# Transformer block with its backward pass on one core: order and pacing of the projection work beside the first chunk of attention

## The chip, the core and the metric

The kernel runs on one core of a Trainium2 chip. The core has five engines that each work through their own instruction list in order and wait for one another by semaphores: PE (TensorE, matmuls and transposes; its weight loads are shown as PEld), DVE (VectorE), ACT (ScalarE), POOL (GpSimd) and SP (SyncE, which here only starts transfers). POOL starts transfers too. The metric is device time in microseconds (us), the median of several runs; lower is better.

## The reference

The program computes one block (attention, then an MLP with squared ReLU, both with adaptive layer norm) and the gradients of all its parameters and of its input. What matters here is the attention of the forward pass: 2048 tokens, width 512, 32 heads of width 16.

```python
qkv = (x @ wqkv).reshape(B, S, 3, H, Dh).transpose(2, 0, 3, 1, 4)
q, k, v = (qkv[0], qkv[1], qkv[2])
scores = jnp.einsum('bhqd,bhkd->bhqk', q, k) * scale
p = _softmax(scores, axis=-1)
o = jnp.einsum('bhqk,bhkd->bhqd', p, v)
...
h = _layernorm(x, axis=-1) * (1 + ca) + sa
x = x + ga * _A_ref(h, A_wqkv, A_wo)
```

Its gradient needs Q, K and V again, in two layouts: with the head channels on the partitions ("feature-major", written by the projections) and with the tokens on the partitions ("token-major", or, for V, the reverse turn). So each projected block is also turned by PE transposes and stored in device memory for the backward pass.

## The kernel before

**Steps and units.** The forward attention goes through chunks of 512 queries (`qc`, 4 of them), in each through 8 groups of four heads (`g`), in each through two pairs of heads (`jp`). One (`qc`, `g`, `jp`) is a unit, numbered `n`; the first chunk is units 0 to 15. A unit has 16 steps (`kb`), one for each block of 128 keys. A step is: two score matmuls on PE into a PSUM tile `st` (L388), one exponential of 128x1024 on ACT into `pu` (L391), and eight small matmuls `pv` of an earlier step on PE into `accbank` (L322). `st` has two buffers.

**Background work.** Only units 0 and 1 have their Q and K ready when attention starts. The others are projected during the first chunk by `gen_qkv` (L663), a Python generator that emits a few PE matmuls and yields what they cost. After each step of units 2 to 15 `bg.step(1.2)` (L405) advances it: it adds 1.2 to a credit (at most 2) and runs the generator until the credit is used up. What the generator yields decides the pacing:

- a number is a price, taken off the credit;
- a tuple stops this step's work. `("wait", n)` also sets `hold` to n, and the next n steps then run no background at all and add no credit (L65 to L67);
- a tuple such as `(g, 0)` or `(-g, 0)` is a mark as well.

`bg.until(mark)` (L382, L408) runs the generator until it passes the mark, whatever that costs, between two steps. It is called twice for each group of heads: in the second unit of group g, ahead of step 5, until the first block of Q of group g+1 is projected (mark g+1); and at the end of that unit until all of K of group g+1 is (mark -(g+1)). In this document such a run between two steps is called a burst. `bg.drain()` (L371) at the end of the first chunk runs what is left.

**What the generator does for a group.** Q block 0, four K blocks (into the tile `KTq` that the next group's scores read), then, for some groups, extra work: the turns of a scaled weight `wm_s` (`gen_turn`, groups 4 to 7), or of V (`gen_vt`, groups 3 to 6), or the modulation rows (`gen_mod`, group 2). Then Q blocks 1 to 3 of the group before.

**One block** is `gen_fm` (L623): four matmuls into a PSUM tile `pps` (L630, a yield of 1 after each of the first three), the evacuation by DVE (L637, "CAST", into `ev_fm` or `KTq`), a store on SP's queue (L641), and then `token_major` (L643): four transposes of that same block into another `pps` tile (L717), its copy by DVE into `ev_tm` (L720), and a store on POOL's queue (L647 for K; L650 and L652 for Q). Between the evacuation and the turn stands `yield ("wait", 1)` (L659). `pps` has two buffers (`self.mps`). For the blocks projected during units 0 and 1 the turns are put in a list, `late`, and done one per step at the start of unit 2.

**V** (`gen_vt`, L694): four token blocks, each padded into a tile `vpad` (a DVE memset of a column of ones, L703, then two POOL `tensor_scalar`, L704 and L705), then `("wait", 3)` (L706), then eight transposes, a copy into `vT`, and after the fourth a store (L708). The column `one` has two buffers.

**Queues.** The orders of PE, ACT, DVE and SP are as the Python code emits them; POOL's order in this stretch is set by a scheduler. `load_q` (L299) loads the next unit's queries on POOL's queue (L302); it comes right after the burst ahead of step 5.

Of the kernel before, what the change touches and what calls it, by code (L numbers as in the profile page):

```python
# [10 lines left out]
F32 = mybir.dt.float32  # L11
ACT = mybir.ActivationFunctionType
ALU = mybir.AluOpType
# [6 lines left out]
P = 128  # L20
DH = 16
# [14 lines left out]
class Background:  # L36
# [13 lines left out]
    def next(self):  # L50
        while self.gens:
            r = next(self.gens[0], None)
            if r is not None:
                if isinstance(r, tuple):
                    self.mark = r[0]
                    self.seen.add(r[0])
                return r
            self.gens.pop(0)
        return None
# [46 lines left out]
class K:  # L106
# [160 lines left out]
    def phase_fwd(self):  # L267
# [66 lines left out]

        KT = kp.tile([P, S], BF16, name="KTq")
        self.late = []
# [3 lines left out]
        QTo = []  # L340
        first = self.gen_open(Vaug, KT, QTm, QTo, stp, bg)
        next(first)
# [5 lines left out]
        for i, (n, kb) in enumerate(units):  # L348
# [4 lines left out]
            for a in range(2):  # L353
                nc.tensor.matmul(stt[:, a, :], lhsT=KT[:, kb * P:(kb + 1) * P], rhs=(QTm[2 + a] if n else QTo[a])[:],
                                 start=True, stop=True)
# [11 lines left out]
        bg.until(-1)  # L367
        KT = self.KT_next
        for n, (qc, g, jp) in list(enumerate(order))[2:]:
# [9 lines left out]
            for kb in range(ST):  # L379
# [7 lines left out]
                for a in range(2):  # L387
                    nc.tensor.matmul(stt[:, a, :], lhsT=KT[:, kb * P:(kb + 1) * P], rhs=QTm[2 * jp + a][:],  # L388
                                     start=True, stop=True)
# [16 lines left out]
            if jp == 1 and n + 1 < len(order):  # L406
                if n < 2 * NQ - 1:
                    bg.until(-(g + 1))  # L408
                KT = KTn
        bg.until(f"fc2_{SC - 2}")  # L410
# [212 lines left out]
    def gen_fm(self, ps, t, g, s0, dst=None, masked=None):  # L623

        nc = self.nc
        DT, NQ = self.DT, self.NQ
        eb = self.qkv_eb
        pt = ps.tile([P, 512], F32, name="pps")
        for kt in range(DT):
            nc.tensor.matmul(pt[:], lhsT=self.wpads[t][:, kt, g, :] if g else self.wpad0[t][:, kt, :], rhs=self.xm1T[:, kt, s0:s0 + 512],  # L630
                             start=(kt == 0), stop=(kt == DT - 1))
            if kt < DT - 1:
                yield 1
        if dst is None:
            ev = eb.tile([P, 512], BF16, name="ev_fm")
            dst = ev[:]
        nc.vector.tensor_copy(dst, pt[:])  # L637
        if masked:
            for j in range(4):
                (nc.scalar.copy if j == 1 else nc.vector.tensor_copy)(masked[j][32 * j:32 * j + 32, :], ev[32 * j:32 * j + 32, :])  # L640
        nc.sync.dma_start((self.QTq_d, self.KTq_d)[t][g, :, s0:s0 + 512], dst)  # L641

        def token_major():  # L643
            tm = eb.tile([P, 4, 4, 32], BF16, name="ev_tm")
            self.turn_now(tm[:].rearrange("p s j e -> p s (j e)"), dst, 4)
            if t:
                nc.gpsimd.dma_start(self.ktm_d[g, :, s0:s0 + 512], tm[:].rearrange("p s j e -> p (s j e)"))  # L647
                return
            tmc = eb.tile([P, 4, 4, DH], BF16, name="ev_tmc")
            nc.gpsimd.tensor_copy(tmc[:], tm[:, :, :, 0:DH])  # L650
            w = 4 * DH
            nc.gpsimd.dma_start(self.qtm_d[g, :, s0 // P * w:(s0 // P + 4) * w],  # L652
                                tmc[:].rearrange("p s j d -> p (s j d)"))

        if self.late is not None:
            self.late.append(token_major)
            yield 1
            return
        yield ("wait", 1)  # L659
        token_major()  # L660
        yield 1.5

    def gen_qkv(self, kp):  # L663

        nc = self.nc
        S, NQ, ST = self.S, self.NQ, self.ST
        for g in range(1, NQ):
            while self.cur_g < g - 1:
                yield ("wait", 0)
            KT = self.KT_next = kp.tile([P, S], BF16, name="KTq")  # L670
            yield from self.gen_fm(self.mps, 0, g, 0)
            yield (g, 0)
            for s0 in range(0, S, 512):
                yield from self.gen_fm(self.mps, 1, g, s0, dst=KT[:, s0:s0 + 512])
            yield (-g, 0)
            if 3 < g <= 3 + self.DT:
                wt = self.qkv_eb.tile([P, 3 * self.DT, P], BF16, name="wm_t", bufs=1)
                yield from self.gen_turn(wt[:], w[:], 3 * self.DT)
                nc.gpsimd.dma_start(self.WmT_d[g - 4], wt[:].rearrange("p n k -> p (n k)"))
            if 2 < g < 3 + self.DT:  # L680
                w = self.qkv_eb.tile([P, 3 * self.D], BF16, name="wm_s", bufs=2)
                sc = self.qkv_eb.tile([P, 1], F32, name="wm_c", bufs=2)
                nc.vector.tensor_copy(sc[:], self.opcaT[:, g - 3:g - 2])
                nc.gpsimd.tensor_scalar(w[:], self.wq[:, g - 3, :], sc[:], 1.0, ALU.mult, ALU.mult)
            if g == 2:
                yield from self.gen_mod()
            elif 3 <= g < 3 + self.SC:
                yield from self.gen_vt(4 * (g - 3))
            for s0 in range(512, S, 512):
                yield from self.gen_fm(self.mps, 0, g - 1, s0)  # L690
        for s0 in range(512, S, 512):
            yield from self.gen_fm(self.mps, 0, NQ - 1, s0)

    def gen_vt(self, s0):  # L694

        nc = self.nc
        NQ = self.NQ
        vT = self.qkv_eb.tile([P, NQ, 4 * P], BF16, name="vT", bufs=1)
        for k in range(4):
            vp = self.vpads[k]  # L700
            v = self.Vaug[:, s0 + k, :, 0:DH].rearrange("p (g j) d -> p g j d", j=4)
            one = self.qkv_eb.tile([P, 1], F32, name="one", bufs=2)
            nc.vector.memset(one[:], 1.0)  # L703
            nc.gpsimd.tensor_scalar(vp[:, :, 0:2, 0:DH], v[:, :, 2:4, :], one[:], 1.0, ALU.mult, ALU.mult)  # L704
            nc.gpsimd.tensor_scalar(vp[:, :, 2:4, 0:DH], v[:, :, 0:2, :], one[:], 1.0, ALU.mult, ALU.mult)  # L705
            yield ("wait", 3)  # L706
            yield from self.gen_turn(vT[:, :, k * P:(k + 1) * P], vp[:].rearrange("p g j e -> p (g j e)"), NQ)
        nc.gpsimd.dma_start(self.VTq_d.rearrange("g p s -> p g s")[:, :, s0 * P:(s0 + 4) * P], vT[:])  # L708

    def gen_turn(self, dst, src, n, pool=None, name="pps", copies=None):  # L710
# [1291 lines left out]
```

## Time and profile before

| | us |
|---|---|
| median of 3 runs (3242.07 to 3249.86) | 3242.19 |
| the profiled execution: its own time | 3241.86 |
| its span, first to last instruction | 3240.1 |
| PE busy | 3034.6 (94%) |
| ACT busy | 2818.9 (87%) |
| DVE busy | 2140.4 (66%) |
| POOL busy | 753.1 (23%) |
| ACT exponentials of L391, 992 of them | 912.8 |
| idle time of ACT just ahead of them | 69.0 |

The profile is of one execution; its own time is 0.33 us below the median. A busy PE is not PE at its peak, since matmuls overlap and their ends are modelled. The change touches only the stretch from the start of unit 2 (the first exponential of L391 starts at 64.21 us) to the end of unit 15 (the next unit's first one starts at 341.10 us); shares over the whole span say little about it.

### The profile page before, as it was taken

The page shows a single profiled execution, that of the slowest core. Times are in us where ns is not written, and L with a number is a line of the kernel's source. Part 1 is how long each engine was busy: PE and PEld are TensorE (multiplying, and loading weights), DVE is VectorE, ACT ScalarE, POOL GpSimd, SP SyncE. Part 2 cuts the span into 40 slices and gives each one's busy share as a digit, 9 for nine tenths or more (in the row PEclk, how much of TensorE's full clock was granted, in tenths as well). Part 3 has the DMA queues.
Part 4 walks back from the last instruction along what each step waited for, and adds up shares of the span by engine and source line. Part 5 has one row for each costly group of instructions (what it writes and reads, how often), then busy time and mean ns, then how long its engine had stood idle before and what let it go on. Part 6 is the DMA issues. An engine that isn't in the chain of part 4 may idle for free.

```text
span 3240.1 us, 86820 instructions
## 1 busy us (share of the span) xinstructions
PE 3034.6 (94%) x35635; PEld 1580.3 (49%) x35879; DVE 2140.4 (66%) x4195; ACT 2818.9 (87%) x4259; POOL 753.1 (23%) x1337
## 2 busy tenths in 40 slices
PE   8888999999999699999999999999999999999998
PEld 4544555555555248444444444444444444444443
DVE  6333223312332657588888888888888888888867
ACT  7876999999999045499999999999999999999965
POOL 3233511211121213421221122122212221221122
PEclk9999999999999899999999999999999999999999
DMA  4122401311221334400000000000000000000033
GB/s 150 60 70 96 134 19 61 99 47 32 101 69 36 99 100 148 142 22 11 12 13 12 13 13 12 13 13 13 13 12 13 13 12 13 13 11 14 20 99 116
DMA packets 76933, 158.53 MB, mean 49 GB/s; under 512 B 15140, under 2 KB 41126, under 8 KB 76534
## 3 DMA queue, kind: packets, MB, share of 16 engines
q0 software_dynamic: 38720, 104.04, 10.3%
q1 hardware_dynamic: 35734, 47.88, 4.5%
q8 instruction: 280, 4.59, 0.6%
q10 hardware_dynamic: 2080, 1.05, 0.1%
q14 instruction: 119, 0.97, 0.1%
HBM read 88.41 MB, written 64.49 MB: 47 GB/s over the span
## 4 chain that ended last, share of the span: by engine, by line
PE 32%; issue 30%; ACT 24%; POOL 8%; DVE 5%; DMA 0%; POOLq 0%; DVEq 0%; ACTq 0%; SPq 0%
ACT pu L391 21%; PE st L1642 5%; POOL ds L1577 4%; PE dp L717 3%; DVE ds L1562 3%; PE st L388 3%; PE st L717 2%; PE acckv L1495 2%; PE dps L1024 1%; PE accbank L322 1%; PE dps L1080 1%; PE accq L1520 1%; PE pps L630 1%; PE dp L1695 1%; PE st L1790 1%
## 5 line engine op out<-in xcount | busy, mean ns | idle before, releaser
L1562 DVE TENSOR_TENSOR ds<-dp,pu 128x512 bf16<-128x512 f32 x1888 | 1226.0, 685 | 137.4 <-PE dp L1558 98.7
L1645 ACT ACTIVATE pu<-st 128x512 bf16<-128x512 f32 x2048 | 1116.5, 611 | 43.9 <-PE dp L1558 15.7
L391 ACT ACTIVATE pu<-st 128x1024 bf16<-128x1024 f32 x992 | 912.8, 1081 | 69.0 <-PE st L388 67.5
L717 PEld LDWEIGHTS <-ds 128*128 128x128 bf16 x8192 | 461.0, 98 | 334.4 <-issue 282.0
L388 PE MATMUL st<-QTm,KTq 128*128 128x512 bf16 x1823 | 552.7, 377 | 37.3 <-ACT pu L391 3.9
L322 PEld LDWEIGHTS <-pu 128*128 128x128 bf16 x8192 | 342.8, 96 | 225.5 <-issue 2.3
L720 ACT COPY dsT<-st 128x1024 bf16<-128x1024 bf16 x416 | 427.2, 1027 | 18.4 <-PE st L717 12.1
L717 PE MATMUL dp<-ident,ds 128*128 128x128 bf16 x4096 | 340.6, 221 | 29.7 <-POOL ds L1577 29.0
L322 PE MATMUL accbank<-Vaug,pu 128*128 128x17 bf16 x8192 | 357.6, 171 | 9.8 <-ACT Vaug L521 1.1
L1577 POOL TENSOR_TENSOR ds<-csq,pu 128x512 bf16<-128x512 f32 x128 | 147.6, 1153 | 939.1 <-ACT csq L1576 939.1
L1642 PE MATMUL st<-kvm,QTg 64*128 64x512 bf16 x1024 | 333.2, 382 | 12.2 <-ACT dsT L720 6.9
L1642 PE MATMUL st<-kvm,q 64*128 64x512 bf16 x1024 | 332.7, 383 | 9.8 <-ACT dsT L720 5.6
L1558 PE MATMUL dp<-kvm,q 64*128 64x512 bf16 x1024 | 337.6, 383 | 1.0 <-PE st L1642 0.7
L1558 PE MATMUL dp<-kvm,dOTg 64*128 64x512 bf16 x1024 | 337.5, 382 | 0.0
L720 DVE COPY dsT<-dp 128x1024 bf16<-128x1024 bf16 x416 | 286.5, 689 | 60.1 <-PE dp L717 49.7
L717 PE MATMUL st<-ident,ds 128*128 128x128 bf16 x4096 | 318.1, 221 | 0.1
L388 PEld LDWEIGHTS <-KTq 128*128 128x128 bf16 x1984 | 186.8, 96 | 157.4 <-issue 122.4
L1495 PE MATMUL acckv<-ds,Qg 128*16 128x512 bf16 x1024 | 175.8, 382 | 0.0
L1495 PE MATMUL acckv<-pu,q 128*16 128x512 bf16 x1024 | 175.8, 382 | 0.0
L1495 PE MATMUL acckv<-ds,q 128*16 128x512 bf16 x1024 | 175.8, 382 | 0.0
L1495 PE MATMUL acckv<-pu,dOg 128*16 128x512 bf16 x1024 | 175.8, 382 | 0.0
L302 POOL DMA_DIRECT2D QTm<-QTq_d x124 | 63.1, 510 | 369.2 <-PE st L388 351.3
(442 smaller groups left out, 3797.2 us busy)
## 6 DMA issues: line engine op xcount, KB each, us to landing
KTq<-KTq_d POOLq DMA_DIRECT2D x24, 512.0 KB, 3.8
duT_d<-auT POOLq DMA_DIRECT2D x3, 1792.0 KB, 7.3
aT_d<-rT POOLq DMA_DIRECT2D x3, 1792.0 KB, 12.2
tm_st<-duT_d SPq DMA_DIRECT2D x14, 384.0 KB, 3.5
tm_st<-aT_d SPq DMA_DIRECT2D x14, 384.0 KB, 3.3
KTq_d<-KTq SPq DMA_DIRECT2D x32, 128.0 KB, 1.8
QTq_d<-ev_fm SPq DMA_DIRECT2D x32, 128.0 KB, 1.9
ktm_d<-ev_tm POOLq DMA_DIRECT2D x32, 128.0 KB, 2.1
```

The source lines that it names most:

```text
L302: nc.gpsimd.dma_start(QTm[j][32 * j:32 * j + 32, :], self.QTq_d[g, 32 * j:32 * j + 32, 512 * qc:512 * (qc + 1)])
L322: nc.tensor.matmul(acc[:, a, sub, :], lhsT=pu[:, a, sub * P:(sub + 1) * P], rhs=Vaug[:, kb, h, :], start=(kb == 0 and a == 0 and sub == 0) ...
L388: nc.tensor.matmul(stt[:, a, :], lhsT=KT[:, kb * P:(kb + 1) * P], rhs=QTm[2 * jp + a][:], start=True, stop=True)
L391: nc.scalar.activation(pu[:], stt[:], ACT.Exp, scale=self.scale)
L717: nc.tensor.transpose(pt[:, i, :], src[:, (b0 + i) * P:(b0 + i + 1) * P], self.ident[:])
L720: (copies or [nc.vector.tensor_copy])[b0 // 8 % len(copies or [0])](dst[:, b0:b0 + m, :], pt[:, :m, :])
L1495: nc.tensor.matmul(acckv[r:r + DH, :], lhsT=T[n][:, ib, col:col + DH], rhs=src[:, a, :], start=(ib == 0), stop=(ib == ST - 1))
L1558: nc.tensor.matmul(dp[:], lhsT=T["dOT"][rd, ib * P:(ib + 1) * P], rhs=masked["VT"][a][rd, 512 * c:512 * (c + 1)], start=True, stop=True)
L1562: nc.vector.tensor_tensor(dsg[:, i, a], dp[:], pu[:, a, :], ALU.mult)
L1577: nc.gpsimd.tensor_tensor(dsg[:, i, 1], f[:], pu[:, 1, :], ALU.mult)
L1642: nc.tensor.matmul(stt[:], lhsT=T["QT"][rs, q], rhs=masked["KT"][a][rs, c0:c0 + 512], start=True, stop=True)
L1645: nc.scalar.activation(pu[:, a, :], stt[:], ACT.Exp, scale=self.scale)
```

## The change

- In `gen_fm` the `("wait", 1)` is gone. Instead there is a `yield 1`, and then the turn of the block *before* this one is emitted (`turn_before`, which keeps one open turn in `tm_open`); this block's own turn follows after the next block's projection.
- The last open turn is emitted at the end of `gen_qkv`.
- The padding of V moves out of `gen_vt` into `pad_v`, which pads all four blocks at once and is called for groups 3 to 6 at the start of the group's work, ahead of the projection of Q block 0. The four `("wait", 3)` are gone.

```diff
@@ -656,18 +656,27 @@
             self.late.append(token_major)
             yield 1
             return
-        yield ("wait", 1)
-        token_major()
-        yield 1.5
+        yield 1
+        yield from self.turn_before(token_major)
+
+    def turn_before(self, nxt):
+
+        for f in self.tm_open:
+            f()
+            yield 1.5
+        self.tm_open = [nxt] if nxt else []
 
     def gen_qkv(self, kp):
 
         nc = self.nc
         S, NQ, ST = self.S, self.NQ, self.ST
+        self.tm_open = []
         for g in range(1, NQ):
             while self.cur_g < g - 1:
                 yield ("wait", 0)
             KT = self.KT_next = kp.tile([P, S], BF16, name="KTq")
+            if 3 <= g < 3 + self.SC:
+                self.pad_v(4 * (g - 3))
             yield from self.gen_fm(self.mps, 0, g, 0)
             yield (g, 0)
             for s0 in range(0, S, 512):
@@ -690,12 +699,11 @@
                 yield from self.gen_fm(self.mps, 0, g - 1, s0)
         for s0 in range(512, S, 512):
             yield from self.gen_fm(self.mps, 0, NQ - 1, s0)
-
-    def gen_vt(self, s0):
+        yield from self.turn_before(None)
+
+    def pad_v(self, s0):
 
         nc = self.nc
-        NQ = self.NQ
-        vT = self.qkv_eb.tile([P, NQ, 4 * P], BF16, name="vT", bufs=1)
         for k in range(4):
             vp = self.vpads[k]
             v = self.Vaug[:, s0 + k, :, 0:DH].rearrange("p (g j) d -> p g j d", j=4)
@@ -703,8 +711,14 @@
             nc.vector.memset(one[:], 1.0)
             nc.gpsimd.tensor_scalar(vp[:, :, 0:2, 0:DH], v[:, :, 2:4, :], one[:], 1.0, ALU.mult, ALU.mult)
             nc.gpsimd.tensor_scalar(vp[:, :, 2:4, 0:DH], v[:, :, 0:2, :], one[:], 1.0, ALU.mult, ALU.mult)
-            yield ("wait", 3)
-            yield from self.gen_turn(vT[:, :, k * P:(k + 1) * P], vp[:].rearrange("p g j e -> p (g j e)"), NQ)
+
+    def gen_vt(self, s0):
+
+        nc = self.nc
+        NQ = self.NQ
+        vT = self.qkv_eb.tile([P, NQ, 4 * P], BF16, name="vT", bufs=1)
+        for k in range(4):
+            yield from self.gen_turn(vT[:, :, k * P:(k + 1) * P], self.vpads[k][:].rearrange("p g j e -> p (g j e)"), NQ)
         nc.gpsimd.dma_start(self.VTq_d.rearrange("g p s -> p g s")[:, :, s0 * P:(s0 + 4) * P], vT[:])
 
     def gen_turn(self, dst, src, n, pool=None, name="pps", copies=None):
```

## The prediction

> **What bounds the kernel now.** First the page's costliest groups. The exponential of the forward attention is one of them, and it is the only large group that stands idle for PE's score matmuls rather than the other way round:
>
> ```profile
> L391 ACT ACTIVATE pu<-st 128x1024 bf16<-128x1024 f32 x992 | 912.8, 1081 | 69.0 <-PE st L388 67.5
> ```
>
> So ACT sets the pace of the forward attention, and 69.0 us of it is lost waiting for scores. Second, the timeline of ACT alone, which tells where (start, duration of the run of exponentials, and in brackets the idle time ahead of it):
>
> ```profile
> 136.96 19.36 ACT L391 ACTIVATE pu<-st 128x1024 bf16<-128x1024 f32 x21 [3.44 <-PE st L388]
> 164.31 10.19 ACT L391 ACTIVATE pu<-st 128x1024 bf16<-128x1024 f32 x11 [8.00 <-PE st L388]
> 177.95 19.36 ACT L391 ACTIVATE pu<-st 128x1024 bf16<-128x1024 f32 x21 [3.44 <-PE st L388]
> 207.84 10.19 ACT L391 ACTIVATE pu<-st 128x1024 bf16<-128x1024 f32 x11 [10.53 <-PE st L388]
> 221.70 19.36 ACT L391 ACTIVATE pu<-st 128x1024 bf16<-128x1024 f32 x21 [3.68 <-PE st L388]
> 252.85 10.19 ACT L391 ACTIVATE pu<-st 128x1024 bf16<-128x1024 f32 x11 [11.79 <-PE st L388]
> 266.72 19.36 ACT L391 ACTIVATE pu<-st 128x1024 bf16<-128x1024 f32 x21 [3.68 <-PE st L388]
> 296.61 10.19 ACT L391 ACTIVATE pu<-st 128x1024 bf16<-128x1024 f32 x11 [10.53 <-PE st L388]
> 310.47 29.44 ACT L391 ACTIVATE pu<-st 128x1024 bf16<-128x1024 f32 x32 [3.68 <-PE st L388]
> 341.10 79.12 ACT L391 ACTIVATE pu<-st 128x1024 bf16<-128x1024 f32 x86 [1.19 <-PE st L388]
> ```
>
> The counts alternate, 21 steps and 11 steps: every gap lies at a burst, at the end of a unit or ahead of step 5, and between bursts ACT runs without a break at 0.92 us a step (19.36 / 21). Two more such gaps lie earlier, 3.23 us ahead of 100.18 us and 3.22 us ahead of 123.29 us. The twelve add up to 66.4 us: all that the change can win. The rest (1.8 us in unit 2, 0.3 us at the modulation columns) is not of bursts. Third, the timeline of all engines inside the burst ahead of 164.31 us:
>
> ```profile
> 157.25 0.40 PE L717 MATMUL pps<-ident,ev_fm 128*128 128x128 bf16 x4 [0.79 <-DVE ev_fm L637]
> ...
> 157.48 1.03 PE L630 MATMUL pps<-xm1T,wpad 128*128 128x512 bf16 x4
> 157.69 0.42 DVE L720 COPY ev_tm<-pps 128x512 bf16<-128x512 bf16 x1 [0.49 <-PE pps L717]
> 158.18 0.40 POOL L650 COPY ev_tmc<-ev_tm 128x256 bf16<-128x256 bf16 x1 [0.59 <-DVE ev_tm L720]
> 158.55 0.69 DVE L637 CAST ev_fm<-pps 128x512 bf16<-128x512 f32 x1 [0.44 <-PE pps L630]
> 158.87 0.57 POOL L652 DMA_DIRECT2D qtm_d<-ev_tmc  x1 [0.29 <-POOL ev_tmc L650]
> 159.30 0.40 PE L717 MATMUL pps<-ident,ev_fm 128*128 128x128 bf16 x4 [0.79 <-DVE ev_fm L637]
> ...
> 159.53 1.03 PE L630 MATMUL pps<-xm1T,wpad 128*128 128x512 bf16 x4
> ```
>
> A block in a burst is a chain: four matmuls 1.03, then 0.79 in which PE waits for the evacuation, then 0.23 until the next block starts (157.25 to 157.48): 2.05 us, as 157.48 to 159.53 shows.
>
> **Prices.** A 512-column matmul starts 0.217 us after the one before ((1.03 - 0.383 of a single one) / 3); the last one's end lies 0.17 beyond the next start. Eight `pv` less are worth 8 x 0.026 = 0.21 (nine last 0.38, one 0.17). From the build's order of PE instructions I took what each burst holds. The one ahead of 136.96 us holds three matmuls, turn, four matmuls, turn: 0.81 + 0.79 + 0.23 + 1.03 + 0.79 + 0.23 = 3.88, and ACT lost 3.44. So a burst's chain costs ACT itself less 0.44 (what lies ready in `st`); with two matmuls for three (3.67 - 0.44 = 3.23) it gives the 3.22 measured. Where the burst's step has one `pv` and not nine, less 0.65.
>
> **Part 1: no holds.** The holds go (one skipped step per block, three per V block), and each block is charged 1 credit more (5.5 for 4.5). In the built order the bursts shrink: where one held up to four blocks of Q and 16 transposes of V, it now holds two or three blocks. The work that leaves them lies in steps. There it must fit under ACT's 0.92. Summed by the prices above (0.43 for the scores, 0.026 a `pv`, 0.217 a matmul, 0.23 four transposes), the 20 steps ahead of each step-5 burst of groups 3 to 6 come to 16.0 to 16.9 us of PE against 18.4 of ACT, where they were 14.0 to 14.3; the fullest stretch is units 4 and 5 at 18.1. The densest stretch of before, ten steps at 8.80, ran with ACT never idle. I cost the move at 0; without that slack every us moved would come back.
>
> **Part 2: turns one block late.** In a burst the turn of the last block fills PE's wait for this block's evacuation, and the next block's matmuls wait for that evacuation because `pps` has two buffers: 1.03 + 0.79 = 1.82 a block, so 0.23 saved each. Larger is the end: after the last block PE issues its four matmuls (0.87) and an older turn (0.23), waits for nothing, and goes on with the scores. In the built order those scores wait only for their `QTm` loads, as the last K block is read 12 steps later. A burst "three matmuls, turn, four, turn" now costs 0.81 + 0.79 + 0.87 + 0.23 - 0.44 = 2.26; a third block adds 1.82: 4.08.
>
> The sum over the twelve bursts of the built order: six of two blocks 13.6; three of three blocks (ahead of step 5 in groups 4, 5, 6 of the list) 12.3; one with two matmuls first and one `pv` 1.84; the first, four matmuls and a turn, 0.87 + 0.23 - 0.65 = 0.45; the drain, two turns with nothing to wait for, 0. Together 28.1. Saved 66.4 - 28.1 = 38.3.
>
> **Part 3: padding ahead of Q block 0.** In DVE's built order four memsets now stand between the copy of the last turn and the evacuation of Q block 0, the last in its burst. The column `one` has two buffers, so the fourth memset waits until POOL has padded the second block. POOL, from the end of that copy: 0.07 and L650 0.40; L704 0.48; the transfer L652 0.57, which the scheduler put between; L705 0.48; L704 and L705 again 0.93: about 2.95, and with the memset (0.06 and the signal) 3.1. Counted from when PE has issued the next-to-last block, that copy ends at 1.35 (0.21 + 0.69 + 0.03 + 0.42), so the last evacuation starts at 4.45 where it would have at 2.04 (0.96 + 0.87 + 0.21): 2.4 late. Behind it on DVE waits the copy of the burst's own turn (nobody is near it) and on PE the first K matmul, one step on, which needs that `pps` buffer: PE stands from about 2.7 to 5.2, `st` runs dry, and ACT, due at 3.6, goes on at 6.05. That is 2.45 us in each of four bursts: 9.8. Moved past on POOL: L650, L652 and two L302 of the next queries, and on SP the Q store; chain 3.1 + 0.7 + store 1.9 + issue 1.0 + landing 2.0 = 8.7, while PE needs the queries 11 steps later (10.1) and after two more stalls. Cost 0, until that chain grows by some 5 us. The padding is off V's own turns, which come 12 to 17 steps later, and takes with it the 1.9 us that PE waited for POOL in the last V block of three bursts (counted in the 66.4). Lower end of this term 0 (the evacuation not held); upper end 17.6, if the evacuation waited for all eight pads (four more at 0.48, 4.4 each).
>
> **The clock.** PE has waited for POOL before, three times alike, and once the granted clock fell to half:
>
> ```profile
> PE pps L717 <- POOL vpad L705: 5.8, 3, 1.9
> 242.30:245.00 2.70, 2.70 (x12) 1.24 (x12) 0.69 (x1) 0.00 (x0) 0.68 (x1) 0.50 0.00 0
> ```
>
> That burst cost 11.79 against 10.53 for the same work: 1.26. Four new waits, longer than 1.9, at one in three give 1.7; bounds 0 and 5.0. The Trainium skill ("TensorE: Matmul & The Clock Gate", section "What's actually happening") puts the fall after an idle window of about 3.4 us; by it these waits cost no clock and the time would be 1.7 less. The trace shows the fall after 1.9, so I keep the row.
>
> **Sum.** 3241.9 - 38.3 + 9.8 + 1.7 = 3215.1; the median stands 0.3 above the profiled execution: 3215.
>
> **Rivals.** *Evacuation not held:* DVE's wait hides, clock stays: 3242.2 - 38.3 = 3204. For it, POOL is only 23% busy; against, DVE's built order. 18%. *Longer stall:* all eight pads and four clock falls: 3242.2 - 38.3 + 17.6 + 5.0 = 3226. For it, a longer wait than the one that already tripped the clock; against, only two buffers' worth of pads is waited for. 14%. *Still held by pacing:* the higher charge leaves the bursts as full as before and only the 0.23 of some 29 burst blocks is won: 3242 - 7 = 3235. The built order speaks against it. 4%. *Slower:* turns and V pieces in steps wait for evacuations as they did in bursts. Some 40 turns and 32 half V turns now lie in steps; at 0.79 each PE pays 57, of which the slack of four 20-step stretches (2 us each) takes 8: 3242 - 38 + 10 + 49 = 3263. It decides from 36 us, about half of all turns waiting. For it, PE sits close to 0.92 in full steps; against, the 19.36 us runs hold such turns with no idle time, and a whole step now lies between evacuation and turn. 4%.
>
> **Numbers.** My case has 60%, own range 3210 to 3221. Faster by over 0.3% (9.7 us, about what a measurement can tell from no change) holds in my case and the first two rivals: 92%; same 4%, slower 4%. The range runs from the first rival to the second: 3204 to 3227.
>
> **What would show it.** In the profile after: twelve gaps ahead of L391 of 2.3 or 4.1 us, none of 8 to 12; in four places a second gap near 2.4 one step after a step-5 burst, with PE waiting on DVE `ev_fm` L637 and DVE waiting on POOL L705 or L713; everything after unit 16 shifted whole. I am wrong if idle time of ACT appears between bursts (PE too full), if the four second gaps are missing or twice as long, or if scores wait for `KTq`.

## The result, and the profile after

| | before | after |
|---|---|---|
| median of 4 runs, us | 3242.13 (3241.38 to 3249.86) | 3221.35 (3216.32 to 3224.56) |
| the profiled execution: its own time | 3241.86 | 3216.32 |
| its span | 3240.1 | 3214.5 |
| ACT's idle time ahead of the exponentials (L391) | 69.0 | 41.9 |
| first score matmul of unit 16 starts at | 340.40 | 311.80 |
| last exponential of the forward attention starts at | 1044.9 | 1018.8 |

The ratio is 0.9929 (95% interval 0.9908 to 0.995): faster. The same kernel in five more runs (*again*, below) had a median of 3222.41, ratio 0.9937 (0.9924 to 0.995). The forecast was 3215, 3204 to 3227. Line numbers of the kernel after are 14 higher from `gen_turn` on (L717 is now L731, the pads L704 and L705 are L712 and L713).

The group of the page that led the prediction, now (busy time and mean, then idle time ahead of it and what ended most of that):

```profile
L391 ACT ACTIVATE pu<-st 128x1024 bf16<-128x1024 f32 x992 | 913.8, 1080 | 41.9 <-PE st L388 38.4
```

The exponentials themselves cost what they did; 27.1 us of the wait is gone. Where, the timeline of ACT in the kernel after shows (start, duration of the unbroken run, what, and in brackets the idle time ahead of it):

```profile
119.84 1.02 ACT L391 ACTIVATE pu<-st 128x1024 bf16<-128x1024 f32 x1 [1.82 <-PE st L388]
123.03 9.27 ACT L391 ACTIVATE pu<-st 128x1024 bf16<-128x1024 f32 x10 [2.17 <-PE st L388]
134.54 19.38 ACT L391 ACTIVATE pu<-st 128x1024 bf16<-128x1024 f32 x21 [2.24 <-PE st L388]
...
194.28 1.02 ACT L391 ACTIVATE pu<-st 128x1024 bf16<-128x1024 f32 x1 [4.05 <-PE st L388]
197.45 9.27 ACT L391 ACTIVATE pu<-st 128x1024 bf16<-128x1024 f32 x10 [2.15 <-PE st L388]
208.96 19.38 ACT L391 ACTIVATE pu<-st 128x1024 bf16<-128x1024 f32 x21 [2.24 <-PE st L388]
...
282.97 137.98 ACT L391 ACTIVATE pu<-st 128x1024 bf16<-128x1024 f32 x150 [2.24 <-PE st L388]
```

The gaps of 8 to 12 us are gone. (Below, an "end burst" is one at the end of a unit, a "step-5 burst" one ahead of step 5.) Bursts of two blocks cost 2.24 to 2.25, bursts of three 4.05 to 4.06. New are runs of a single exponential: behind it stands a second gap of 2.15 to 2.17, four in all, one step after each step-5 burst of groups 3 to 6. The runs of 21 steps are unbroken at 19.38, so nothing that left the bursts shows up between them.

A second gap from the inside, in the timeline of all engines of the kernel after:

```profile
154.26 0.41 DVE L734 COPY ev_tm<-pps 128x512 bf16<-128x512 bf16 x1
...
154.62 0.07 DVE L711 MEMSET one<- 128x1 f32 x2
...
156.17 1.02 ACT L391 ACTIVATE pu<-st 128x1024 bf16<-128x1024 f32 x1 [2.25 <-PE st L388]
156.19 0.49 POOL L713 TENSOR_SCALAR vpad<-Vaug,one 128x256 bf16<-128x256 bf16 x1
156.65 0.47 POOL L712 TENSOR_SCALAR vpad<-Vaug,one 128x256 bf16<-128x256 bf16 x1
156.74 0.06 DVE L711 MEMSET one<- 128x1 f32 x1 [2.05 <-POOL vpad L713]
157.11 0.47 POOL L713 TENSOR_SCALAR vpad<-Vaug,one 128x256 bf16<-128x256 bf16 x1
...
157.64 0.06 DVE L711 MEMSET one<- 128x1 f32 x1 [0.85 <-POOL vpad L713]
157.69 0.69 DVE L637 CAST ev_fm<-pps 128x512 bf16<-128x512 f32 x1
...
158.43 0.38 PE L630 MATMUL pps<-xm1T,wpad 128*128 128x512 bf16 x1 [2.15 <-DVE ev_fm L637]
```

Read it from the end. PE's first K matmul stood 2.15 for a `pps` buffer. That buffer was free only when DVE had evacuated Q block 0 (157.69). DVE could not, because ahead of that evacuation in its order stand two memsets that waited 2.05 and 0.85 for POOL to finish pads that still read `one`. POOL's work in between is 0.5 us a piece. An engine of which 23% is busy over the whole span sets the end here.

**The time lost later.** At unit 16 the kernel is 28.6 us ahead (340.40 - 311.80), at the last exponential 26.1. At the first ACT work of the MLP that follows (the copy to `fT`, 1136.99 before, 1114.37 after) it is 22.6, at the end 25.6. Two waits lie behind the first chunk that were not there before. POOL's timeline, first after:

```profile
839.99 0.53 POOL L302 DMA_DIRECT2D QTm<-QTq_d  x1 [11.01 <-PE st L388]
840.51 0.59 POOL L309 DMA_DIRECT2D KTq<-KTq_d  x1
841.09 0.51 POOL L302 DMA_DIRECT2D QTm<-QTq_d  x1
841.64 0.70 POOL L1335 TENSOR_SCALAR lnb_gp<-x,lnb_nc1r 128x512 f32<-128x512 bf16 x1
```

and before:

```profile
867.99 0.69 POOL L1321 TENSOR_SCALAR lnb_gp<-x,lnb_nc1r 128x512 f32<-128x512 bf16 x1 [10.81 <-DVE lnb_nc1r L1317]
868.64 0.54 POOL L302 DMA_DIRECT2D QTm<-QTq_d  x1
869.17 0.59 POOL L309 DMA_DIRECT2D KTq<-KTq_d  x1
869.76 0.51 POOL L302 DMA_DIRECT2D QTm<-QTq_d  x1
```

The step of the layer norm's gradient stood ahead of three loads and now stands behind them, 1.65 us later (841.64 - 839.99). Its result feeds a turn that PE has to do before the next scores; the timeline of PE in the kernel after:

```profile
843.94 0.61 PE L731 MATMUL pps<-ident,dxb 128*128 128x128 bf16 x4 [1.27 <-DVE dxb L1292]
```

and the stretch that follows (start and end, length, busy time of PE, PEld, DVE, ACT and POOL with the number of instructions, the granted clock of PE (1.00 is full), the share of the DMA engines, GB/s):

```profile
844.00:846.00 2.00, 2.00 (x17) 1.17 (x18) 0.42 (x1) 0.51 (x1) 0.00 (x0) 0.50 0.51 184
```

The clock is at half here, and ACT loses 1.65 and 0.50 at 844. The second place comes right after the last exponential. PE's timeline after, and the stretch behind it:

```profile
1020.04 1.98 PE L731 MATMUL pps<-ident,xh 128*128 128x128 bf16 x16 [1.15 <-DVE xh L1246]
```

```profile
1022.00:1026.00 4.00, 3.22 (x9) 1.13 (x8) 1.44 (x2) 0.00 (x0) 0.46 (x1) 0.50 0.39 135
```

and PE's timeline before:

```profile
1045.25 1.77 PE L717 MATMUL pps<-ident,xh 128*128 128x128 bf16 x16 [0.23 <-DVE xh L1232]
```

The wait is 1.15 for 0.23, and the clock falls to 0.50 for some six us, in which PE gets through 9 matmuls in 4 us; before, the stretch at the same place shows 16 at a clock of 1.00. The 56 matmuls behind the turns of `xh` took 15.62 us for 13.08; with the 0.92 of longer wait that is the loss of 3.5 between the last exponential and `fT`.

### The profile page after: what moved, and what is told of

Same layout as the page of the kernel before. It is cut to its first block, busy times and chain, and to the rows that moved or that the text cites. A ratio compares the mean times of both kernels' runs of the same rounds, so it can differ in the third digit from the quotient of the medians.

```text
span 3214.5 us, 86824 instructions
## 1 busy us (share of the span) xinstructions
PE 3025.6 (94%) x35633; PEld 1582.0 (49%) x35879; DVE 2138.1 (67%) x4195; ACT 2819.6 (88%) x4259; POOL 753.7 (23%) x1337
## 4 chain that ended last, share of the span: by engine, by line
PE 31%; issue 31%; ACT 24%; POOL 8%; DVE 5%; DMA 1%; POOLq 0%; DVEq 0%; ACTq 0%; SPq 0%
ACT pu L391 21%; PE st L1656 5%; POOL ds L1591 4%; PE dp L731 3%; PE st L388 3%; DVE ds L1576 3%; PE st L731 2%; PE acckv L1509 2%; PE accbank L322 1%; PE dps L1094 1%; PE accq L1534 1%; PE dp L1709 1%; PE pps L630 1%; PE st L1804 1%; PE dps L1038 1%
## 5 line engine op out<-in xcount | busy, mean ns | idle before, releaser
L391 ACT ACTIVATE pu<-st 128x1024 bf16<-128x1024 f32 x992 | 913.8, 1080 | 41.9 <-PE st L388 38.4
L731 PEld LDWEIGHTS <-ds 128*128 128x128 bf16 x8192 | 460.5, 98 | 333.7 <-issue 281.4
L731 PE MATMUL dp<-ident,ds 128*128 128x128 bf16 x4096 | 340.2, 221 | 29.8 <-POOL ds L1591 29.0
L731 PE MATMUL st<-ident,ds 128*128 128x128 bf16 x4096 | 317.7, 220 | 0.1
```

The costliest lines, as they stand in the source:

```text
L391: nc.scalar.activation(pu[:], stt[:], ACT.Exp, scale=self.scale)
L731: nc.tensor.transpose(pt[:, i, :], src[:, (b0 + i) * P:(b0 + i + 1) * P], self.ident[:])
```

## Experiments

All edits are made on the kernel after; unless said otherwise times are medians and ratios are against the kernel before, run on the same chip.

**again: the kernel after, unchanged.**

> The changed kernel once more, for its spread and a second profile. Theory A (half-clock windows after short PE waits make the spread): the profiled first chunk has the same gaps (2.2, 4.05, second gaps 2.15), each either as before or about 1 us longer where the granted clock fell; the gap near the 844 us mark and the long idle time after the last exponential come back, since the order makes them. Times between 3216 and 3225, low clock with long time. Rival (the later loss of 3 us is an accident of one execution): those two places show nothing.

3222.41 (3218.58 to 3223.92). The profiled execution (3223.92) had the same twelve bursts and the same waits of PE, but the clock fell after two of the four second gaps (same view and columns as above):

```profile
124.00:128.00 4.00, 3.93 (x36) 1.90 (x36) 0.07 (x1) 2.73 (x3) 1.55 (x5) 0.59 0.18 53
162.00:166.00 4.00, 3.78 (x32) 2.07 (x32) 0.80 (x2) 2.76 (x3) 2.19 (x5) 0.57 0.26 70
```

Each cost ACT 1.03 to 1.07 in shorter gaps close behind (0.25 + 0.50 + 0.28 and 0.36 + 0.71). In the profile of the first run it fell after none. So one profile shows what the orders of work do, and not how often the clock falls.

**ones4: four buffers for the column of ones**, so that no memset waits.

```diff
-            one = self.qkv_eb.tile([P, 1], F32, name="one", bufs=2)
+            one = self.qkv_eb.tile([P, 1], F32, name="one", bufs=4)
```

> Column of ones with four buffers instead of two, so no memset waits for POOL. Theory (the last evacuation of the burst is held by the third and fourth memset): the four second gaps of 2.15 to 2.17 us vanish, everything else in the first chunk stays; 8.6 us less than the changed kernel, 3208 for an execution without clock falls in the first chunk, median near 3212. Rival (POOL or the port it shares with DVE holds the evacuation): second gaps stay at over 1 us.

3210.11 (3209.95 to 3213.4), ratio 0.9903 (0.9888 to 0.9918): 12.3 us less than *again*. ACT's timeline:

```profile
120.75 10.21 ACT L391 ACTIVATE pu<-st 128x1024 bf16<-128x1024 f32 x11 [1.82 <-PE st L388]
...
190.70 10.21 ACT L391 ACTIVATE pu<-st 128x1024 bf16<-128x1024 f32 x11 [4.04 <-PE st L388]
```

The runs of 1 and 10 steps have become runs of 11 and the bursts ahead of them are what they were. The second gaps were 8.6 together. The other 3.7 of the 12.3 are not traced; clock falls behind the second gaps, two of about 1 us in the profile of *again*, would be part of it. The run-to-run spread is narrower (3.5 us for 5.3), but over four and five runs that says little.

**ones1: one buffer**, to double the suspected wait.

```diff
-            one = self.qkv_eb.tile([P, 1], F32, name="one", bufs=2)
+            one = self.qkv_eb.tile([P, 1], F32, name="one", bufs=1)
```

> One buffer for the column of ones instead of two: the fourth memset now waits for the third block's padding, one block (0.93 us on POOL) more. Theory: each second gap grows from 2.15 to about 3.1 us, 3.7 us in the first chunk in all, and clock falls come after more of the four. Rival (the gap is not made by the memsets' wait): still 2.15.

3230.9 (3227.31 to 3236.14), ratio 0.9958 (0.9947 to 0.997), with the kernel before at 3246.18 on that chip. The second gaps grew, to 4.27, 3.70, 3.70 and 3.70, more than the 3.1 expected. ACT's timeline at one of them:

```profile
160.93 1.02 ACT L391 ACTIVATE pu<-st 128x1024 bf16<-128x1024 f32 x1 [2.25 <-PE st L388]
...
165.65 2.17 ACT L391 ACTIVATE pu<-st 128x1024 bf16<-128x1024 f32 x2 [3.70 <-PE st L388]
...
168.53 1.02 ACT L391 ACTIVATE pu<-st 128x1024 bf16<-128x1024 f32 x1 [0.71 <-PE st L388]
```

The expectation left out that with one buffer POOL in turn waits for each memset (12 times, 3.5 us): DVE waited for POOL 12 times, 17.5 us, where the kernel after has 8 waits and 11.6. The clock fell after all four.

**pad_late: the padding later**, behind the last K block of the group and its mark `(-g, 0)`, so that it stands behind the evacuations of Q block 0 and of all four K blocks.

```diff
-            if 3 <= g < 3 + self.SC:
-                self.pad_v(4 * (g - 3))
...
             yield (-g, 0)
+            if 3 <= g < 3 + self.SC:
+                self.pad_v(4 * (g - 3))
```

> The padding, all four blocks at once and with two buffers of ones, moved behind the last K block of the group instead of ahead of Q block 0; PE's order is that of the changed kernel. Theory (what costs is that an evacuation stands behind the memsets, not the padding): no second gaps in groups 4 to 6, where the turns of the scaled weight come first, and one of about 1 us at most in group 3, where V is turned at once; 7 to 8 us less than the changed kernel, 3208 to 3215. Rival (V's turns now wait for POOL as they did before): gaps of 2 us stay at V's first turn in each group.

3211.05 (3209.35 to 3216.46), ratio 0.9905 (0.9886 to 0.9924), near *ones4*. In groups 4 to 6 there is no second gap. In group 3 there is another, of 2.09 where at most 1 was expected; PE's timeline there:

```profile
134.83 0.40 PE L731 MATMUL pps<-ident,vpad 128*128 128x128 bf16 x4 [2.07 <-POOL vpad L713]
```

V's first turn now comes before its pad is ready. So padding early has a use. The 2.15 needs two things together, and each of these two runs takes one away: too few buffers of ones (*ones4*), and an evacuation behind the memsets in DVE's order (*pad_late*, still with two buffers).

**realign: the credit at the start of the second chunk set to what it was before the change.** At the end of the first chunk the kernel before leaves a credit of -0.1, the kernel after one of -1.25, which puts the background work that follows one step back.

```diff
                 bg.drain()
+                bg.credit = -0.1
                 es.close()
```

> The changed kernel with the credit set to -0.1 after the drain, the value that the kernel before had there; the order of all background work after the first chunk is then that of before. Theory (the 3.1 us that the shift lost later come from the MLP work standing one step later: POOL's loads ahead of L1335, and the last layer norm behind the last exponential, each with a PE wait and a clock fall): the gap near 844 us and the half clock after the last exponential vanish, and the gain of 28.7 us at unit 16 is kept to the end: 3213 without clock falls, 3 us less than the changed kernel. Rival (clock falls come anyhow with the phase of the clock's window): same time as the changed kernel, within its spread.

3214.01 (3213.58 to 3220.17), ratio 0.9917 (0.9901 to 0.9933): 8.4 less than *again*. Timeline of ACT, and of PE after the last exponential:

```profile
286.95 734.45 ACT L392 ACTIVATE pu<-st 128x1024 bf16<-128x1024 f32 x800 [2.24 <-PE st L389]
```

```profile
1020.63 1.77 PE L732 MATMUL pps<-ident,xh 128*128 128x128 bf16 x16 [0.23 <-DVE xh L1247]
```

All 800 exponentials behind the first chunk's last burst run without a break; the wait ahead of the turns is 0.23 again, and the clock four us on is 1.00. The two waits are those of the shifted order, then. Over all thirteen profiles: PE waited 1.14 to 1.15 there in all six with the shifted order (after, *again*, *ones4*, *ones1*, *own_turn*, *pad_late*) and 0.23 in all seven with the order of before. The gain in the medians (8.4) is larger than the 6.0 that the profile after lost between unit 16 and the `fT` copy (28.6 - 22.6). That difference stays open: clock falls differ between executions, and only one execution of each was profiled. The interval of the ratio also just touches that of *again* (0.9901 to 0.9933 against 0.9924 to 0.995). And in its own profile *realign* does not win the second loss back whole: from the end of the last exponential to the `fT` copy it took 93.4 us, for 91.0 before and 94.5 after, with the clock at half for longer further on (14 matmuls behind the first turn of `dxb` took 5.95 for 4.73), behind PE waits of 3.4 to 3.8 that the kernel before has too. Over the seven profiles with the order of before this stretch took 90.4 to 94.8, over the six with the shifted one 93.7 to 98.2.

**ones4_realign: both edits.**

> Both edits. Theory: they add, 3204 to 3206, 36 to 38 us under the kernel before, with the narrowest spread of the four, since four waits of PE over 2 us and the two later ones are gone. Rival: the gains overlap, over 3209.

3204.69 (3202.32 to 3211.75), ratio 0.9888 (0.987 to 0.9905). Within the spread the two add up (12.3 and 8.4 from 3222.41 would be 3201.7), as would be expected of causes far apart in time. On top of *ones4*, though, the credit is worth 5.4 and not 8.4, and the intervals of these two ratios overlap; the narrower spread that was expected did not come.

**own_turn: holds out, but each block turned right after its own evacuation**, to part the two halves of the change.

```diff
         yield 1
-        yield from self.turn_before(token_major)
+        token_major()
+        yield 1.5
```

> The changed kernel, but each block's own turn follows its evacuation again (after a yield of 1, no hold). Theory (the late turn shortens bursts: the end of a burst waits for no evacuation): two-block bursts go back to 3.4 us, three-block ones to 5.5 to 5.7, about 14 us more in the first chunk in all; 3230 us against 3216 for an execution without clock falls. Rival (taking the holds out is what counts): bursts of the same length as in the changed kernel and 3216 to 3224.

3249.95 (3246.29 to 3253.76) against 3246.61 of before on that chip: ratio 1.0012 (1.0001 to 1.0022), no gain at all, where 3230 was expected. The end bursts came out as priced, 3.24 to 3.48. The waits of PE (in total, times, longest) say where the rest went:

```profile
PE pps L732 <- DVE ev_fm L637: 26.5, 21, 3.4
PE pps L732 <- DVE KTq L637: 12.0, 17, 0.8
```

With no hold between evacuation and turn, PE waits for its evacuation 38 times, 38.5 us; the kernel before has 31 such waits, 24.3 us, all at bursts. Most of the difference is the padding: four waits of 3.35 to 3.37 (13.4 us) ahead of the step-5 bursts of groups 3 to 6, where the held evacuation is that of the block to be turned, and the clock fell to half after all four. The step-5 bursts grow to 5.6 to 8.7. Outside the bursts PE waits 11 times, 5.8 us in all. So the mechanism of the prediction's "slower" rival exists as soon as the turns are not late, but far from its size: the rival put 57 us on turns in steps. The first exponential of unit 16 starts 4.5 us later than before (345.56 for 341.10). Leaving out the holds, with V padded early, gains nothing by itself; the late turn is needed beside them. What it would gain without the held evacuation (own turns with four buffers of ones) was not run.

**holds_back: late turns, but with the hold in each block.**

```diff
-        yield 1
+        yield ("wait", 1)
         yield from self.turn_before(token_major)
```

> The changed kernel with the hold of one step per block put back in place of the yield of 1; turns still a block late, V still padded first. The order of the work after the first chunk then falls on that of before. Theory (the higher charge of 5.5 takes back what the hold gave, so this part is worth nearly nothing): bursts of two and three blocks as in the changed kernel, first chunk within 3 us of it, and the later loss gone: 3213 to 3218. Rival (the holds kept the background from running): bursts of three and four blocks, 3230 or more.

3218.79 (3218.73 to 3218.84), ratio 0.9916 (0.9897 to 0.9935). Two runs only. The bursts: 1.68, 2.02, 2.24, 2.25, 2.25, 4.29, 2.24, 4.29, 2.25, 4.28, 2.24, 1.40, together 31.4 for 27.9, and one second gap grew from 2.17 to 3.21. It ends no later than the kernel after, whose order behind the first chunk costs it more than that. Once the turn is late, leaving out the hold of a block is worth 3.5 us in bursts, a little more than the 3 expected; against 38.5 for the whole change that is little.

**vholds: the hold of three steps put back ahead of each V block's turn.**

```diff
         for k in range(4):
+            yield ("wait", 3)
             yield from self.gen_turn(
```

> The changed kernel with the hold of three steps ahead of each V block put back (padding still at the start of the group). The order after the first chunk falls on that of before. Theory (the twelve skipped steps a group are what filled the step-5 bursts): four step-5 bursts hold four blocks and V turns, 6.6 us in group 3 and about 7.1 in groups 4 to 6 against 2.25 and 4.05; 13 us more in the first chunk, 3224 in all. Rival (the padding's place is what counts, not the holds): bursts as in the changed kernel, 3211 to 3216.

3233.27 (3230.99 to 3240.36), ratio 0.997 (0.9954 to 0.9985), 12 more than the kernel after. ACT's timeline ahead of two step-5 bursts:

```profile
160.81 1.02 ACT L391 ACTIVATE pu<-st 128x1024 bf16<-128x1024 f32 x1 [6.49 <-PE st L388]
...
202.11 1.02 ACT L391 ACTIVATE pu<-st 128x1024 bf16<-128x1024 f32 x1 [7.25 <-PE st L388]
```

These gaps (2.25 and 4.05 in the kernel after; 6.6 and 7.1 expected) are what the V holds did: twelve steps in which no background ran, made up in one burst. Unit 16 starts 18 us later than after, where 13 were expected; a clock fall (1.04), a second gap of 1.65 and a drain of 0.96 are most of the rest. The end moved by less (12), and the order behind the first chunk is that of before here, without its two waits.

**ones4_rate and rate18: a higher rate, so that bursts have less to catch up.**

```diff
-                rate = 1.14 if qc else 1.2
+                rate = 1.14 if qc else 1.45
...
-            one = self.qkv_eb.tile([P, 1], F32, name="one", bufs=2)
+            one = self.qkv_eb.tile([P, 1], F32, name="one", bufs=4)
```

(`rate18` has 1.80 for 1.45.)

> Four buffers for the column of ones, and a rate of 1.45 instead of 1.2 in the first chunk. The order after it falls on that of before. By the prices of the prediction the bursts now hold none to two blocks, 12 us in all against 28, while PE comes to 17.6 of 18.4 us in most stretches and 0.2 to 0.6 us over ACT's time in four: theory 3191, 13 us under ones4_realign. Rival (PE has no room left in steps; what leaves the bursts comes back as idle time between them): 3202 to 3206.

> Four buffers of ones and a rate of 1.8 in the first chunk: all but two of the twelve bursts hold no whole block any more. By the prices PE then has 19.0 to 19.8 us of work in stretches where ACT has 18.4. Theory (PE becomes the bound in steps, so the rest of the burst time comes back as short idle times between exponentials): 3188 to 3193, no clear gain over the rate of 1.45. Rival (steps still have room): 3182 or less.

1.45: 3193.64 (3189.73 to 3195.97), ratio 0.984 (0.9827 to 0.9854). 1.80: 3191.0 (3188.92 to 3193.3), ratio 0.9838 (0.9823 to 0.9853). Both beat both kernels. ACT's timeline at 1.45:

```profile
160.56 19.38 ACT L391 ACTIVATE pu<-st 128x1024 bf16<-128x1024 f32 x21 [1.00 <-PE st L388]
```

```profile
182.39 10.58 ACT L391 ACTIVATE pu<-st 128x1024 bf16<-128x1024 f32 x11 [2.46 <-PE st L388]
```

The end bursts fall from 2.24 to 1.00 and the step-5 bursts from 4.05 to 2.46, by 1.24 and 1.59, less than the price of a block (1.82). Runs of 21 steps mostly still take 19.38, but those of 11 take 10.58 to 10.66 for 10.21: PE begins to bind in the fullest steps. At 1.80 the timeline reads

```profile
105.65 31.64 ACT L391 ACTIVATE pu<-st 128x1024 bf16<-128x1024 f32 x32 [0.38 <-PE st L388]
137.67 31.41 ACT L391 ACTIVATE pu<-st 128x1024 bf16<-128x1024 f32 x32 [0.38 <-PE st L388]
```

Here the step-5 bursts are gone and the end bursts cost 0.38, but a step takes 0.99 (31.64 / 32) and not 0.92. PE is now full in the steps, and the work that leaves the bursts comes back there. Between the two no difference can be told (the intervals overlap).

## Why the prediction was right, and where it failed

- **Bursts.** Twelve gaps were priced at 28.1 and measured 27.9: 0.45, 1.82, six of 2.24 to 2.25, three of 4.05 to 4.06, the drain none. The chain per block and the count of blocks from the built order were both right. Nearby kernels came close to the same prices: *holds_back*'s three-block bursts were 4.28 to 4.29, and the bursts of *ones4_rate* come to nearly 13 us where 12 were expected.
- **Part 1 at 0.** Right: 19.38 for 21 steps, unbroken. *vholds* shows which holds mattered (V's), *rate18* where the slack that the term counted on ends. *own_turn* shows that the term is 0 only with Part 2.
- **Part 3.** Mechanism and place were right, with the size a little high: 2.45 each, 9.8 together, against 2.15 to 2.17, 8.6. DVE's delay was as priced: 3.02 from the end of the last turn's copy to the evacuation (154.67 to 157.69), for 3.1. The missing 0.3 is on ACT's side: the exponential ahead of the gap ended 2.52 after that copy (157.19), where 3.6 - 1.35 = 2.25 had been counted, so ACT was due later. *ones4* takes the buffers away as the cause and the gaps go; *ones1* makes them longer.
- **The clock.** One in three at 1.26 was about right: 7 of 20 such waits over five kernels, at 0.9 to 1.2 each where the cost can be read apart (0 of 4 in the profile after, 2 of 4 in *again*).
- **The sum to unit 16.** 38.3 less 9.8 is 28.5; measured 28.6. That they agree so closely is partly luck: 38.5 from the bursts less 8.6 for the second gaps would be 29.9, and 1.3 went in places that were not priced, 0.5 of it in small gaps before 102 us (2.6 for 2.1). The 1.7 for the clock did not arise in this profile.
- **The step that failed** is "everything after unit 16 shifted whole". Of 28.6 only 26.1 are left at the last exponential and 22.6 at the next ACT work. The prediction costed nothing behind the first chunk. But the new prices leave another credit at its end, and that moves the planner's background work against the scores and POOL's loads. It cost two waits of PE and, in this profile, two clock falls. *realign* shows that the waits come from the credit; how much of the 6.0 does is not settled, since the stretch behind the last exponential varies by some 4 us from profile to profile in one and the same order. The stretch from the `fT` copy to the end took 2103.1 us before and 2100.1 after (3240.1 - 1136.99, 3214.5 - 1114.37); over the profiles of the same work it varies between 2100 and 2106, so those 3.0 us belong to the profiled execution, not to the change.
- **The median** of 3221.35 is 5.0 above the profiled execution of the kernel after, where the prediction added the 0.3 of before. It lies inside the forecast's 3204 to 3227 but 0.35 above the central case's own 3210 to 3221; of the 6 us above 3215 this term is 4.7. The profiled execution alone came out 1.2 above the sum (3216.32 for 3215.1): 3.0 lost behind unit 16, less the 1.8 by which unit 16 came earlier than the whole sum (26.8) had it. What sets single runs apart was not seen; the granted clock goes with it (0.992 at 3216.32, 0.989 at 3224.56), and the falls at the second gaps are about 1 us each.
- **The rivals.** "Evacuation not held" is what *ones4_realign* brings about on purpose: 3204.69 against its 3204. "Longer stall" needed all eight pads; four were waited for, those of two blocks. "Still held by pacing" and "slower" did not come, but *own_turn* shows that the latter's waits exist, at 5.8 us outside the bursts and not 57.

## What to carry to other kernels

Where an engine waits for another's evacuation inside a burst, do the piece of work that depends on it one block later: the wait is then filled with the next block, and pacing that was there to hide it can go. Holds are not free: those ahead of V's turns alone cost 11 to 12 us when put back. Before work is moved ahead on an in-order engine, count the buffers of its smallest tile: a column of 128 ones with two buffers cost 12 us of 3222. And when prices or holds of a planner are changed, look at what it leaves behind at the end of the stretch: a credit that differs by 1.15 moved work by a step 500 and 700 us later.

## What the runs showed of the hardware

The granted clock fell to half after short waits of PE, and not every time: after 1.27 (near 844 us) in 2 of 6 profiles (*ones4*, *ones1*, *own_turn* and *pad_late* lost 1.0 there with no fall), after 1.92 in 1 of 3 in the kernel before, after 2.1 to 2.3 in 7 of 20, and after 3.35 to 3.70 in 8 of 8 (*own_turn*, *ones1*). The same wait of the same kernel can do it or not. Behind the last exponential it fell in all six profiles with the wait of 1.15 ahead of the turns of `xh`, and in one of the seven with 0.23 (*ones4_realign*). There 16 transposes follow the wait, and in five of the six the clock fell while they ran; what part they have in it was not tested. In the kernel after the low clock then lasts some six us. The Trainium skill ("TensorE: Matmul & The Clock Gate", section "What's actually happening") gives an idle window of about 3.4 us, free-running, for the fall. That the outcome changes from run to run agrees with a free-running window; that a wait of 1.27 to 2.3 us can suffice does not agree with a window of full idleness, and here the rows decide.
